# One tile of the first transform, stored as 96 rows to 96 rows instead of four groups of 24

## The chip, the cores and the metric

The kernel runs on one core of one Trainium2 chip. The metric is the device time of one execution in microseconds, lower is better; the time shown for a kernel is the median of its runs. A core has a matrix engine (TensorE, PE in the rows, with PEld for its weight loads), VectorE (DVE), ScalarE (ACT), GpSimd (POOL), a queue engine (SyncE, SP) that here issues nearly all transfers, and 16 DMA engines that carry them. SBUF is the on-chip memory of 128 partitions; a tile's rows lie on partitions.

## What is computed

The input x is [8, 3072, 256]. Along the 3072 positions a real Fourier transform is taken, a complex 256 by 256 matrix mixes the channels, a soft threshold is applied, the inverse transform follows, and the result goes through a feed-forward network with softplus:

```
X = rfft(x, axis=1);  Xr, Xi = X.real, X.imag
Yr = Xr @ w_r - Xi @ w_i + b_r
Yi = Xr @ w_i + Xi @ w_r + b_i
Y  = shrink(Yr) + 1j * shrink(Yi)          # sign(v) * max(|v| - 0.01, 0)
y  = irfft(Y, n=3072, axis=1)
h  = y.reshape(24576, 256) @ w_in          # w_in 256 x 2048
out = softplus(h) @ w_out                  # w_out 2048 x 256
```

## The kernel before

The length 3072 is split as 96 x 32 (N1 x N2). For each of the 8 batches b the spectral part runs in steps that are spread between the feed-forward products of the batch before:

- `s1(b, c)`, c = 0..15: one product with the 96 x 96 matrix `f` gives two of the 32 columns n for all 96 rows, a tile of 96 x 512. ScalarE copies it out of PSUM (L260). Batch 0 keeps all of it on chip, in the tile `a0` (96 partitions, 32 x 256 each). Every other batch stores the tile to a DRAM tensor `a_dr[b]` of [96, 32, 256] (L264, issued in the helper at L100). The first ten tiles of batch 1 come early and go through four slots `a1`, so that tile c may only be copied once the store of tile c - 4 has landed.
- `load_a(b, gp)`, gp = 0..11: fetches two groups g of four rows each, laid out as 128 partitions (four rows times 32 columns n) of 256 values. For batch 0 these are two transfers per step out of `a0` (L273, from SBUF to SBUF, 128 KB each, 24 in all); for the others one transfer out of `a_dr[b]` (L276), beside a table `g1` (L275). The tile `ap` has three buffers, so the transfers of step gp wait until `s3` of step gp - 3 is done.
- `s3` (L287) multiplies by that table, `mix` (L208 to L210) mixes the channels, DVE and POOL apply the threshold, `s4` (L427) begins the inverse transform and its result goes to `d_dr[b]`; `load_d` and `s5` (L455) finish it. Then the feed-forward slots run (`psc`, `pse`, `pso` in the rows).

The columns of `f` do not stand in natural order. They are built on the host as four runs of 24, so that row 24q + g of a tile holds the natural column 4g + q:

```
f = f.reshape(N1, NG, 4).swapaxes(1, 2).reshape(N1, N1)      # NG = 24
```

The four rows of group g are therefore rows g, g + 24, g + 48 and g + 72 of `a0`, and the store to `a_dr` puts them back into natural order, as four groups of 24 rows.

All of these transfers and the streams of weights are issued by SP, one after the other, in an order that a slot plan written out in the kernel fixes (`fill`, `steps`, `later`). In the first 130 us the feed-forward weights are also loaded, split into two parts (`split_w`, L143 to L195) and written back to DRAM (`w_dr`), in between the steps of batch 0. A transfer waits for the one eight places before it on SP to have landed, beside the waits for its data and buffers.

## Time and profile before

| what | us |
|---|---|
| median of 3 runs | 2681.06 |
| lowest and highest run | 2678.23, 2682.66 |
| span of the profiled execution | 2678.0 |
| of it, PE busy | 2603.8 |
| first feed-forward product starts | 131.07 |

The page gives of the profiled execution its span only, 2678.0 us; the lowest run is 0.2 us and the median 3.1 us above it. So what lies around the span is small, and a sum made against the span is carried to the median by adding 3.1 us.

The page's busy shares are averages over the whole span. The first tenth of the run is another regime than the rest, so views of single stretches are read beside it: the table of windows (busy time of each engine in a stretch, the granted clock, the mean busy share of the 16 DMA engines, and what they moved per second), the timeline (instructions in order of time), and the lists of waits.

### The profile page before, as it was taken

Reading aid. Unit: us, or ns where it says so; the run is one execution under the profiler, and the core shown is the slowest. Engines: PE = TensorE matmul, PEld = TensorE weight load, DVE = VectorE, ACT = ScalarE, POOL = GpSimd, SP = SyncE. Lnnn points to the kernel's source line nnn. Section 1 sums busy time; section 2 is a strip of 40 time slices with the busy share of each in tenths; the row PEclk is TensorE's granted clock in tenths of the full one; section 3 lists DMA queues with packets and bytes.
Section 4 is the critical chain, followed back from the end, with each engine's and each line's share of the span. In section 5 each row is a group of like instructions: output and inputs, shape, how many; then the busy total and the mean of one; then the engine's idle time right before and its main releaser. Section 6 shows DMA issues by size and latency. Waiting matters only on the chain.

```text
span 2678.0 us, 36264 instructions
## 1 busy us (share of the span) xinstructions
PE 2603.8 (97%) x13059; PEld 2184.2 (82%) x13059; DVE 1626.2 (61%) x2701; ACT 1719.5 (64%) x3115; POOL 301.3 (11%) x292
## 2 busy tenths in 40 slices
PE   7768999999999999999999999999999999999999
PEld 5546888888888888888888888888888888888887
DVE  3666665666646666566665666556665666645454
ACT  3365666666666666666676666666666666666665
POOL 2432110110101101101011011010010000000000
PEclk8889999999999999999999999999999999999999
DMA  6766556556455565564555644646455455445543
GB/s 191 254 210 206 194 164 198 166 187 193 157 188 178 178 198 170 179 205 156 184 172 172 217 159 153 220 163 198 164 167 191 155 170 188 142 154 183 186 147 110
DMA packets 186116, 479.73 MB, mean 179 GB/s; under 512 B 18097, under 2 KB 86961, under 8 KB 185937
## 3 DMA queue, kind: packets, MB, share of 16 engines
q1 hardware_dynamic: 185376, 476.95, 55.1%
q8 instruction: 103, 1.69, 0.3%
q0 software_dynamic: 560, 0.47, 0.1%
q14 instruction: 77, 0.62, 0.1%
HBM read 390.31 MB, written 83.89 MB: 177 GB/s over the span
## 4 chain that ended last, share of the span: by engine, by line
PE 88%; DVE 2%; DMA 2%; ACT 1%; issue 0%; POOL 0%; SPq 0%; DVEq 0%; ACTq 0%; POOLq 0%
PE pso L208 13%; PE pso L209 12%; PE pso L210 12%; PE psc L208 6%; PE psc L210 6%; PE psc L209 6%; PE pse L208 5%; PE pse L210 5%; PE pse L209 5%; PE psf L455 4%; PE psf L209 4%; PE psf L208 4%; PE psf L210 4%; PE psf L287 2%; DMA w_dr<-wp 1%; DVE shrunk L413 0%
## 5 line engine op out<-in xcount | busy, mean ns | idle before, releaser
L553 DVE TENSOR_TENSOR gl<-t,gh 128x512 fp32r<-128x512 f32 x768 | 533.2, 694 | 349.7 <-ACT gh L547 346.8
L532 ACT COPY t<-psc 128x512 f32<-128x512 f32 x576 | 337.0, 585 | 504.4 <-PE psc L210 502.4
L537 DVE TENSOR_TENSOR t<-pse,t 128x512 f32<-128x512 f32 x576 | 396.2, 688 | 426.9 <-ACT t L532 278.3
L208 PE MATMUL pso<-gh,w 128*128 128x512 f32 x1536 | 616.2, 401 | 0.0
L209 PE MATMUL pso<-gl,w 128*128 128x512 f32 x1536 | 600.0, 391 | 0.0
L210 PE MATMUL pso<-gh,w 128*128 128x512 f32 x1536 | 599.5, 390 | 0.0
L547 ACT CAST gh<-t 128x512 fp32r<-128x512 f32 x768 | 476.8, 621 | 58.2 <-PE pso L210 34.4
L543 ACT ACTIVATE t<-t 128x512 f32<-128x512 f32 x576 | 364.5, 633 | 58.7 <-DVE t L537 58.0
L210 PEld LDWEIGHTS pso<-gh,w 128*128 128x128 f32 x1536 | 288.7, 188 | 62.5
L208 PEld LDWEIGHTS pso<-gh,w 128*128 128x128 f32 x1536 | 290.1, 189 | 54.9
L209 PEld LDWEIGHTS pso<-gl,w 128*128 128x128 f32 x1536 | 290.0, 189 | 51.4
L208 PE MATMUL psc<-y_sb,w 128*128 128x512 f32 x768 | 301.6, 393 | 16.1 <-DMA w<-w_dr 7.8
L210 PE MATMUL psc<-y_sb,w 128*128 128x512 f32 x768 | 300.1, 391 | 0.0
L209 PE MATMUL psc<-y_sb,w 128*128 128x512 f32 x768 | 299.6, 390 | 0.0
L208 PE MATMUL pse<-y_sb,w 128*128 128x512 f32 x576 | 227.8, 396 | 14.4 <-DVE t L537 7.9
L115 POOL TENSOR_TENSOR xl<-xt,xh 96x512 fp32r<-96x512 f32 x102 | 134.1, 1317 | 938.3 <-ACT xh L106 783.6
L209 PE MATMUL pse<-y_sb,w 128*128 128x512 f32 x576 | 225.2, 391 | 0.0
L210 PE MATMUL pse<-y_sb,w 128*128 128x512 f32 x576 | 225.1, 391 | 0.0
L489 POOL TENSOR_TENSOR y_sb<-raw,y_sb 128x512 fp32r<-128x512 f32 x69 | 92.3, 1337 | 1128.5 <-ACT y_sb L486 1124.9
L208 PEld LDWEIGHTS psc<-y_sb,w 128*128 128x128 f32 x768 | 144.5, 188 | 51.0 <-ACT t L532 10.2
L210 PEld LDWEIGHTS psc<-y_sb,w 128*128 128x128 f32 x768 | 144.6, 188 | 31.0
L209 PEld LDWEIGHTS psc<-y_sb,w 128*128 128x128 f32 x768 | 144.6, 188 | 29.7
(131 smaller groups left out, 3637.8 us busy)
## 6 DMA issues: line engine op xcount, KB each, us to landing
w<-w_dr SPq DMA_DIRECT2D x192, 896.0 KB
w<-w_dr SPq DMA_DIRECT2D x192, 512.0 KB
dp<-d_dr SPq DMA_DIRECT2D x80, 384.0 KB
xt<-in_x SPq DMA_DIRECT2D x128, 192.0 KB
d_dr<-d SPq DMA_DIRECT2D x96, 256.0 KB
out_y<-ot SPq DMA_DIRECT2D x96, 256.0 KB
ap<-a_dr SPq DMA_DIRECT2D x84, 256.0 KB
a_dr<-a SPq DMA_DIRECT2D x102, 192.0 KB
```

Of the source, the lines that this page charges most:

```text
L115: (eng or nc.vector).tensor_tensor(out=lo, in0=src, in1=hi.bitcast(F32), op=ALU.subtract)
L208: nc.tensor.matmul(ps, wh, xh, start=start, stop=False, skip_group_check=more)
L209: nc.tensor.matmul(ps, wh, xl, start=False, stop=False, skip_group_check=more)
L210: nc.tensor.matmul(ps, wl, xh, start=False, stop=stop, skip_group_check=more)
L287: nc.tensor.matmul(xv[:, g, k], t[:, g, k * P:(k + 1) * P], g1_t[:, g].rearrange("p (c s) -> p c s", c=2), start=True, stop=True,)
L455: nc.tensor.matmul(ps[:, t - blk * BLK:t - blk * BLK + n], d_sb[b, blk // 2, n2 // 4][0][:, n2 % 4, k * P:(k + 1) * P], d_sb[b, blk // 2, ...
L489: eng.tensor_tensor(out=lo, in0=raw[j], in1=hi.bitcast(F32), op=ALU.subtract)
L532: nc.scalar.copy(t, banks[bank])
L537: nc.vector.tensor_tensor(out=t, in0=banks[bank], in1=t, op=ALU.add)
L543: nc.scalar.activation(t, banks[bank] if bank else t, AF.Softplus)
L547: nc.scalar.copy(gh, ct[key, what])
L553: nc.vector.tensor_tensor(out=gl, in0=ct.pop((key, what)), in1=gh.bitcast(F32), op=ALU.subtract)
```

## The change

Three lines change. The reordering of the columns of `f` is left out, so that row r of a tile is the natural column r. The store of a tile to `a_dr` then writes 96 rows to 96 rows. The four rows of group g in `a0` are now rows 4g to 4g + 3, and `load_a` of batch 0 reads those. The contents of `a_dr` and everything read from it are as before.

```
--- before.py
+++ after.py
         else:
-            store(a_dr[b][:, 2 * c:2 * c + 2, :].rearrange("(g q) n c -> q g n c", q=4), a.rearrange("p (n c) -> p n c", n=2), ("a", b))
+            store(a_dr[b][:, 2 * c:2 * c + 2, :], a.rearrange("p (n c) -> p n c", n=2), ("a", b))
...
             for g in range(2):
-                nc.sync.dma_start(t[:, g, :], a0[2 * gp + g::NG])
+                nc.sync.dma_start(t[:, g, :], a0[4 * (2 * gp + g):4 * (2 * gp + g) + 4])
...
     f[:, 1] = cos(1536 * n1)
-    f = f.reshape(N1, NG, 4).swapaxes(1, 2).reshape(N1, N1)
```

No instruction is added, removed or moved on any engine. On SP, early in the program, the loads of batch 0 (`ap<-a`, L273) and the first stores of batch 1 (`a_dr<-y`, L100) stand in a row like this, with weights, a table and the biases between them:

```order
 L273 DMA ap<-a_79 128x1x256 x6
 L143 DMA w_216<-in_w_in 128x2x512
-L100 DMA a_dr<-y_80 4x24x512
+L100 DMA a_dr<-y_80 96x512
 L273 DMA ap<-a_79 128x1x256 x2
 L749 DMA bias_99<-in_bias 128x512
-L100 DMA a_dr<-y_80 4x24x512 x3
+L100 DMA a_dr<-y_80 96x512 x3
 L273 DMA ap<-a_79 128x1x256 x2
 L749 DMA y_80<-in_g 128x1536
```

Only the shape of the stores differs here; the source rows of the loads differ too, which these rows do not show.

## Rows read from the trace of the kernel before

**Rows 1.** The page: span, then busy time, share and instructions of each engine.

```profile
span 2678.0 us, 36264 instructions
PE 2603.8 (97%) x13059; PEld 2184.2 (82%) x13059; DVE 1626.2 (61%) x2701; ACT 1719.5 (64%) x3115; POOL 301.3 (11%) x292
```

**Rows 2.** Windows: stretch, length, busy of PE, PEld, DVE, ACT, POOL, clock, DMA share, GB/s.

```profile
0.00:280.00 280.00, 217.09 (x1018) 166.56 (x1019) 166.06 (x283) 137.33 (x250) 84.38 (x85) 0.88 0.65 212
280.00:2678.00 2398.00, 2386.71 (x12043) 2017.60 (x12041) 1460.11 (x2418) 1582.12 (x2866) 216.95 (x207) 1.00 0.54 175
```

**Rows 3.** Waits of PE, 20 to 100 us: who for whom, us, times, longest.

```profile
PE psf L287 <- DMA ap<-a: 6.5, 5, 4.3
PE psf L210 <- DVE w L115: 5.6, 2, 4.8
```

**Rows 4.** Windows of short stretches in the first 91 us, columns as in rows 2.

```profile
26.00:30.00 4.00, 2.06 (x8) 1.79 (x8) 0.38 (x1) 0.00 (x0) 0.00 (x0) 0.50 0.28 97
37.00:44.00 7.00, 2.23 (x17) 2.03 (x16) 2.37 (x5) 1.36 (x3) 1.16 (x1) 0.91 0.28 103
3.00:8.00 5.00, 4.10 (x5) 1.48 (x6) 0.00 (x0) 0.94 (x2) 0.00 (x0) 1.00 0.95 261
46.00:47.00 1.00, 1.00 (x7) 1.00 (x7) 0.38 (x1) 0.00 (x0) 0.48 (x1) 0.50 0.99 366
26.00:91.00 65.00, 54.44 (x352) 48.86 (x353) 45.01 (x76) 21.78 (x43) 29.13 (x31) 0.87 0.59 193
```

**Rows 5.** Timeline of SP, 1 to 38 us: start, length, line, transfer, count.

```profile
1.20 17.58 SPq L231 DMA_DIRECT2D xt<-in_x  x20
...
20.84 7.17 SPq L273 DMA_DIRECT2D ap<-a  x6
...
29.41 0.66 SPq L100 DMA_DIRECT2D a_dr<-y  x1
30.39 2.13 SPq L273 DMA_DIRECT2D ap<-a  x2
32.58 2.35 SPq L749 DMA_DIRECT2D bias<-in_bias  x1
35.04 2.98 SPq L100 DMA_DIRECT2D a_dr<-y  x3
```

**Rows 6.** The full list of transfers: count, size of each.

```profile
ap<-a SPq DMA_DIRECT2D x24, 128.0 KB
...
a_dr<-y SPq DMA_DIRECT2D x10, 192.0 KB
```

**Rows 7.** Timeline of PE, `s3` of batch 0 and the first feed-forward product.

```profile
27.83 2.53 PE L287 MATMUL psf<-y,ap 128*128 128x128 f32 x8 [4.25 <-DMA ap<-a]
...
53.49 1.06 PE L287 MATMUL psf<-y,ap 128*128 128x128 f32 x8
...
58.11 1.06 PE L287 MATMUL psf<-y,ap 128*128 128x128 f32 x8
...
90.12 1.33 PE L287 MATMUL psf<-y,ap 128*128 128x128 f32 x8
...
131.07 0.77 PE L208 MATMUL psc<-y_sb,w 128*128 128x512 f32 x1
```

**Rows 8.** Timeline of ACT, 112 to 129 us, with idle time before and its end.

```profile
125.88 0.58 ACT L260 COPY y<-psf 96x512 f32<-96x512 f32 x1 [12.38 <-DMA a_dr<-y]
127.75 0.58 ACT L260 COPY y<-psf 96x512 f32<-96x512 f32 x1 [1.29 <-DMA a_dr<-y]
128.23 0.58 ACT L474 CAST y_sb<-psf 128x512 fp32r<-128x512 f32 x1
```

**Rows 9.** Issue time on SP in ns, least, median, greatest.

```profile
L100 SPq DMA_DIRECT2D a_dr<-a x102: 592/612/925, 155.2 to 2052.1; - x102
...
L231 SPq DMA_DIRECT2D xt<-in_x x128: 312/382/2282, 1.2 to 2027.0; - x128
```

## The prediction

> **What bounds the kernel now.** I read the page first: PE is busy 2603.8 of 2678.0 us [rows 1]. The windows then split the span. From 280 us to the end PE works 2386.7 of 2398 us, so some 11 us are lost in nine tenths of the run; in the first 280 us it works 217.1, so 63 us are lost there [rows 2]. What a transfer costs can therefore show at the start; later there are 11 us to win at the very most, and a transfer would have to become much slower before PE felt it. So the stretch to look at is the one in which batch 0 is read back from `a0`, beside the tiles of batch 1 that are stored early. It runs from 27.8 us, the first product of `s3`, to 90.1 us, its last step; the first feed-forward product follows at 131.1 [rows 7].

> In that stretch PE waits first for the loads `ap<-a`: 6.5 us in five waits, and 5.6 us for a result of DVE [rows 3]. That is little, but the transfers have hardly any slack. The reader should look at the DMA share in the short windows. Between 26 and 30 us, when only the loads issued from 20.8 us on are under way [rows 5], the 16 DMA engines are busy 0.28 on the mean and move 97 GB/s. Between 37 and 44 us, with stores and loads in turn, it is the same picture, 0.28 and 103 GB/s. When tiles of all 128 partitions come in, the share is 0.99 and the pace 366 GB/s [rows 4]. So a load out of `a0` and a store to `a_dr` run on about 4 of the 16 engines, each at some 97/4 = 24 to 103/4 = 25.8 GB/s.

> [...]

> One queue carries all of this. A load of 128 KB [rows 6] takes 131,072 B / 97 GB/s = 1.35 us, and a store of 192 KB takes 196,608 B / 103 GB/s = 1.91 us. From 26 to 91 us, 65 us x 193 GB/s = 12.55 MB move [rows 4]. 24 loads are 3.15 MB of it and 32.4 us; the four stores issued by 38 us [rows 5] are 0.79 MB and 7.6 us; the other 8.61 MB at 366 GB/s are 23.5 us. The sum is 63.5 of 65 us. **The four engines that the loads use are full through the whole stretch.** PE's own step is shorter: where it isn't held up, `s3` of one step follows that of the step before by 58.11 - 53.49 = 4.62 us [rows 7], while two loads and the rest of the queue cost 65/12 = 5.4.

> **The change, part by part.**

> *The reordered table `f`* is made on the host. Nothing of it runs on the chip.

> *The store of a tile* goes from 4 x 24 rows to 96 rows. The nearest row is the load of x, 96 rows of the same size on the same queue, twenty from 1.2 us on [rows 5]: between 3 and 8 us the engines are busy 0.95 at 261 GB/s [rows 4], so 0.75 us for one, against 1.91 now. That saves 1.16 us for each of 102 + 10 stores [rows 6, 9]. The 4 in the full stretch give back 4 x 1.16 = 4.6 us. Two more end a wait of ACT: tiles 8 and 9 of batch 1 are copied at 125.88 and 127.75 us, after 12.4 and 1.3 us of waiting for earlier stores, and the copy that the first feed-forward product's inputs come from is right behind, at 128.23 [rows 8]. Two stores in a row before it give 2 x 1.16 = 2.3 us. The others lie in a stretch where PE loses next to nothing [rows 2]; I take 0 for them, 6 at most. SP needs 612 ns to issue a store and 382 ns for the like-shaped load of x [rows 9]; SP spends its time waiting for PE in that part, so this is worth nothing.

> *The load out of `a0`* keeps its size, its four engines and its place on SP, but its four source rows, until now 24 apart, become neighbours. The trace has no transfer that reads four neighbouring rows, so I bound it. From below: neighbours share nothing, 1.35 us as now. From above: the four engines read through one path, and that path carries what one engine was seen to carry, 24 GB/s: 4 x 1.35 = 5.40 us. The row that decides between the ends is the load of x again. Its engines are busy 0.95 and yet move 261/(16 x 0.95) = 17 GB/s each, where those that load 128 rows move 366/(16 x 0.99) = 23 [rows 4]. Both come from the same memory in long rows; what differs is which partitions they touch. So something on the side of SBUF that belongs to partitions holds engines back, and I take the upper kind of price, with the best pace of an engine seen, 25.8 GB/s, for the path: 131,072 / 25.8 = 5.09 us a load.

> [...]

> With 5.09 us the 24 loads take 122.2 us instead of 32.4, so +89.8, and the stores give back 4.6: the last step of batch 0 comes 85.2 us later. Three buffers of `ap` don't hide that: two loads take 10.2 us a step, against PE's 4.62, and PE's step at half clock, at most 9.2, is still the shorter. What is late next is everything behind the last step; nothing of the feed-forward part can begin before. Two things soften it: the 2.3 us of ACT's wait, and that the splitting of weights and the threshold, which keep DVE busy 45.0 of these 65 us [rows 4], are spread over 150 us and are done when the last step comes. I take 4 us for that, between 0 and 10; a lower clock after the long wait for loads works the other way.

> **Sum.** 85.2 - 2.3 - 4 = +78.9 us on the span of 2678.0, so 2756.9; the median lies 3.1 above the span, so 2760 us. This case's own range, with 4.6 to 5.6 us a load and the softening from 0 to 12, is 2740 to 2780.

> **The rivals.**

> *Neighbours cost nothing.* Then the loads stay at 1.35 us, only the stores count, and the kernel is faster. The price: 4.6 us out of the full queue, of which about half shows, since PE's 4.62 us step is close behind, 2.3 us at ACT, and up to 3 us later: 4 to 8 us, 2675 us. It decides as soon as a load stays under about 1.5 us. For it: now the four engines each read from one row at full pace, so a single row is no obstacle. Against it: the slow engines in the load of x.

> [...]

> *Half the price.* The two loads of a step read two different sets of four rows. If the engines drift apart, so that some are at the first set and some at the second, two paths work at once and a load takes 2.55 us: 61 instead of 32.4, so +28.8 - 4.6 - 6.3 = +18 us, 2699 us. Against it: all four get the loads in the same order and are held up alike.

> *The change doesn't do what it says*: the stores stay on four engines. Then 6.9 us fewer are given back, 2767 us. Against it: the load of x has the same 96 rows and a share of 0.95 [rows 4].

> **How the numbers follow.** Forecast 0.72, neighbours cost nothing 0.16, half the price 0.10, stores unchanged 0.02. The range has to reach down to the half price and leaves out the rival on the other side: 2690 to 2790 us, its upper end for a path slower than one engine. A measurement of this kernel can tell about 0.2%, 5.4 us, from no change. The rival that is faster gives 4 to 8 us, so 0.10 of its 0.16 are faster by more than that and 0.06 lie within; all else is slower, 0.84.

> **What would show it.** Right: the windows of the first 150 us show a DMA share near 0.25 with about 26 instead of 97 GB/s, because four engines are busy and wait for one path; PE's waits for `ap<-a` grow from 6.5 to about 80 us or more; `s3` of batch 0 ends near 175 us, with 10 to 12 us between steps; the first feed-forward product starts near 210; from there to the end the length is as now. The stores, where they run alone, show a share near 0.9 instead of 0.27, and ACT's wait at L260 shrinks. Wrong: `s3` of batch 0 still ends near 90 us, or windows with loads alone still move 97 GB/s. If `s3` ends late but the end moves by much less, the step that failed is that everything behind it shifts by as much.

## The result

The changed kernel takes 2712.6 us, the median of four runs, against 2680.9 us before: a ratio of 1.0117, 95% interval 1.0105 to 1.013. It is slower by 31.7 us, where 79 were forecast. The sign is right, but the size is less than half of what was said. The time lies inside the stated range of 2690 to 2790 us only because that range was drawn down to the rival "half the price"; the forecast's own range was 2740 to 2780.

The profiled execution of the changed kernel has a span of 2705.4 us. Its windows (stretch, length, busy time of PE, PEld, DVE, ACT and POOL with counts, clock, DMA share, GB/s) answer to [rows 2, 4]:

```profile
26.00:30.00 4.00, 0.91 (x4) 0.93 (x4) 0.69 (x1) 0.38 (x1) 0.00 (x0) 0.67 0.24 50
52.40:53.60 1.20, 1.20 (x6) 1.20 (x7) 1.17 (x3) 0.00 (x0) 0.48 (x1) 0.50 0.22 26
62.50:65.50 3.00, 3.00 (x23) 2.52 (x22) 2.93 (x4) 2.70 (x5) 1.35 (x1) 1.00 0.23 52
26.00:125.00 99.00, 61.41 (x355) 53.45 (x356) 43.59 (x77) 21.95 (x44) 28.96 (x31) 0.79 0.45 128
310.00:2705.00 2395.00, 2385.71 (x12046) 2018.60 (x12044) 1461.17 (x2420) 1582.71 (x2867) 217.20 (x207) 1.00 0.54 175
```

From 26 to 30 us the loads out of `a0` are alone on the queue, as before. The share is still that of four busy engines, 0.24 against 0.28, but 50 GB/s move instead of 97 [rows 4]. For a short while, from 52.4 to 53.6 us, the pace is 26 GB/s, that of one engine; at other times it is twice that. The whole stretch that took 65 us for 193 GB/s now takes 99 us at 128 GB/s: nearly the same bytes, 12.5 and 12.7 MB. From 310 us on, PE loses 9.3 of 2395 us, no more than before [rows 2].

PE's waits between 20 and 130 us (who for whom, us in total, times, longest), to be set beside [rows 3]:

```profile
PE psf L287 <- DMA ap<-a: 32.0, 14, 4.6
PE psf L210 <- DVE w L115: 7.0, 1, 7.0
```

And PE's timeline (start, length, instruction, idle before and what ended it), beside [rows 7]: in 14 places PE now waits for the load of one half of an `s3`, where it waited in 5, the last step starts 31.7 us later (121.84 against 90.12), and the first feed-forward product 32.8 us later (163.91 against 131.07).

```profile
29.09 1.20 PE L287 MATMUL psf<-y,ap 128*128 128x128 f32 x4 [4.56 <-DMA ap<-a]
33.02 1.22 PE L287 MATMUL psf<-y,ap 128*128 128x128 f32 x4 [2.73 <-DMA ap<-a]
...
111.07 0.68 PE L287 MATMUL psf<-y,ap 128*128 128x128 f32 x4 [2.77 <-DMA ap<-a]
115.80 1.22 PE L287 MATMUL psf<-y,ap 128*128 128x128 f32 x4 [4.04 <-DMA ap<-a]
...
121.84 0.61 PE L287 MATMUL psf<-y,ap 128*128 128x128 f32 x4
...
163.91 0.77 PE L208 MATMUL psc<-y_sb,w 128*128 128x512 f32 x1
```

So the place and the kind of the cost are as forecast. What has to be explained is why a load that should cost 5.1 us costs much less. With the prediction's own terms, 23.5 us for the other transfers and 3.0 us for the four stores, the 99 us leave (99 - 26.5) / 24 = 3.0 us a load.

### The profile page after: what moved, and what is told of

Its sections match the earlier page's. It is cut to its first block, busy times and chain, and to the rows that moved or that the text cites. A ratio compares the mean times of both kernels' runs of the same rounds, so it can differ in the third digit from the quotient of the medians.

```text
span 2705.4 us, 36264 instructions
## 1 busy us (share of the span) xinstructions
PE 2609.3 (96%) x13059; PEld 2189.8 (81%) x13059; DVE 1625.6 (60%) x2701; ACT 1719.5 (64%) x3115; POOL 301.4 (11%) x292
## 4 chain that ended last, share of the span: by engine, by line
PE 88%; DVE 2%; DMA 1%; ACT 1%; issue 0%; POOL 0%; SPq 0%; DVEq 0%; ACTq 0%; POOLq 0%
PE pso L208 13%; PE pso L209 12%; PE pso L210 12%; PE psc L208 6%; PE psc L210 6%; PE psc L209 6%; PE pse L208 5%; PE pse L210 5%; PE pse L209 5%; PE psf L455 4%; PE psf L209 4%; PE psf L208 4%; PE psf L210 4%; PE psf L287 3%; DVE shrunk L413 0%; DMA w<-in_w_in 0%
```

## The experiments

Three theories went in. **A**: four neighbouring rows share one path that carries what one engine carries, about 26 GB/s; engines that run apart from each other get to different loads, whose rows lie on different paths, and that is where the price fell from 5 to 3 us. **B**: a path simply carries 50 GB/s. **C**: the load isn't the cause.

### The load by itself

A kernel that does nothing but move data: one load, then seven in a row, for several choices of four rows, each block after the end of the one before. A block has a name, the first row of each of its loads, and the distance between the four rows of a load.

```
block("near", [0] * 7, 1)                        # rows 0, 1, 2, 3, seven times
block("far", [0] * 7, 24)                        # rows 0, 24, 48, 72
block("near_next", [0, 4, 0, 4, 0, 4, 0], 1)     # 0-3 and 4-7 in turn
block("near_over", [0, 32, 0, 32, 0, 32, 0], 1)  # 0-3 and 32-35 in turn
block("two_apart", ..., 2); four_apart: 4; eight_apart: 8; most_apart: 32
```

> The disputed cost by itself: a kernel that leaves the whole computation out and only moves data, with nothing beside it. Loads of 128 KB from four rows of SBUF to 128 partitions, in blocks, each block waiting for the one before: one load, then seven in a row, from four neighbouring rows (near), from rows 24 apart (far), from neighbours in turn from two sets (rows 0 to 3 and 4 to 7: near_next; rows 0 to 3 and 32 to 35: near_over), and from rows 2, 4, 8 and 32 apart; then seven stores of 192 KB as four groups of 24 rows and as 96 rows. Theory A (four neighbours share one path of about 26 GB/s, the pace of one engine, and in the changed kernel engines that drift onto the other set of a step use a second path): near 5.1 us a load, so about 36 us for seven, far 1.35 us, so about 10; near_next between, 2.6 to 4 us a load; 2 apart 2.6, 4 apart and more 1.35. [...] Theory B (a path carries about 50 GB/s, whatever the engines do): near 2.6 us a load, 18 us for seven, near_next and near_over the same. Theory C (the load is not what became slow): near as far, about 10 us. Stores: 1.9 us each in groups, 0.5 to 0.75 us as 96 rows.

DVE reads one column of every tile when it has landed; its timeline gives the landings, here the first and the last of seven, neighbours and then rows 24 apart:

```profile
30.80 0.15 DVE L38 COPY flag<-near 128x1 f32<-128x1 f32 x1 [7.11 <-DMA near<-src]
...
62.00 0.15 DVE L38 COPY flag<-near 128x1 f32<-128x1 f32 x1 [4.98 <-DMA near<-src]
...
65.46 0.15 DVE L38 COPY flag<-far 128x1 f32<-128x1 f32 x1 [3.25 <-DMA far<-src]
...
73.95 0.15 DVE L38 COPY flag<-far 128x1 f32<-128x1 f32 x1 [1.25 <-DMA far<-src]
```

Six loads from the same neighbours take 31.20 us, **5.20 us each**; six from rows 24 apart 8.49 us, 1.42 each. The windows of the blocks (here busy times of DVE and POOL, clock, DMA share, GB/s), in the order near, far, near_next, near_over, two, four, eight and 32 apart:

```profile
31.00:62.00 31.00, 0.77 (x6) 0.00 (x0) 1.00 0.21 25
65.50:73.50 8.00, 0.89 (x6) 0.00 (x0) 1.00 0.26 90
81.00:100.00 19.00, 0.86 (x6) 0.00 (x0) 1.00 0.22 39
108.00:138.00 30.00, 0.92 (x6) 0.00 (x0) 1.00 0.22 26
143.00:157.00 14.00, 0.82 (x6) 0.00 (x0) 1.00 0.23 53
161.00:170.00 9.00, 0.92 (x6) 0.00 (x0) 1.00 0.25 82
174.00:182.00 8.00, 0.82 (x6) 0.00 (x0) 1.00 0.26 89
187.00:203.00 16.00, 0.92 (x6) 0.00 (x0) 1.00 0.23 47
```

The share hardly differs, 0.21 to 0.26: in each block four engines count as busy, whether they move 25 or 90 GB/s. Read with theory A, one path carries 25 to 26 GB/s (four neighbours), two carry 53 (rows 2 apart) and four 82 to 90 (rows 4, 8 and 24 apart). B and C fall here. With two sets of neighbours in turn (0 to 3 and 4 to 7) the pace is 39 GB/s, and it grows within the block: the gaps between landings are 5.0, 4.6 and 4.3 us, then 1.4, 1.5 and 3.1. With rows 0 to 3 and 32 to 35 in turn there is no such gain: 26 GB/s, and gaps of 4.7 to 5.3 us to the last.

The same run stores seven tiles in four groups of 24 rows and then seven as 96 rows. The grouped ones land 1.9 to 2.1 us apart and the others, queued up behind them, 0.5 us apart (from the semaphore records that are explained further down); the prediction's sum had 1.91 and 0.75.

### Each half of the change alone

A second order of the columns of `f`, used by batch 0 alone, separates the two halves. The edits that follow are against the changed kernel and cut to their main lines; both also load the second table (72 KB instead of 36 KB) and let batch 0 use it. The store half:

```
+    f_0 = f[:, np.arange(N1).reshape(NG, 4).T.reshape(-1)]
...
-                nc.sync.dma_start(t[:, g, :], a0[4 * (2 * gp + g):4 * (2 * gp + g) + 4])
+                nc.sync.dma_start(t[:, g, :], a0[2 * gp + g::NG])
```

> The store half of the change alone: the table f has a second order of columns that batch 0 alone uses, so batch 0's rows stay 24 apart while the other batches are stored as 96 rows to 96 rows. It loads a table of 72 KB instead of 36 KB at the start. Theories A and B: the cost goes, and what is left is the stores' gain, 4 to 8 us by the prediction, so 2673 to 2677 us. Theory C (the slower part comes from the stores or from the natural order of f): about 2710 us.

2670.7 us, ratio 0.9963 (0.995 to 0.9975): **faster than both kernels**, by 9.9 us or 0.37% (from the ratio) against the kernel before, a little more than the 4 to 8 us that the prediction gave the stores. The last step of batch 0 begins at 88.4 us:

```profile
88.37 1.06 PE L287 MATMUL psf<-y,ap 128*128 128x128 f32 x8
...
130.07 0.77 PE L208 MATMUL psc<-y_sb,w 128*128 128x512 f32 x1
```

The load half keeps natural order for batch 0 and goes back to four groups of 24 for the rest:

```
+    f_0 = f[:, np.arange(N1)]
+    f = f[:, np.arange(N1).reshape(NG, 4).T.reshape(-1)]
...
-            store(a_dr[b][:, 2 * c:2 * c + 2, :], a.rearrange(...), ("a", b))
+            store(a_dr[b][:, 2 * c:2 * c + 2, :].rearrange("(g q) n c -> q g n c", q=4), a.rearrange(...), ("a", b))
```

> The load half alone: batch 0 in natural order, its four rows of a group neighbours, while the other batches keep the reordered columns and the store in four groups of 24. Theories A and B: as slow as the whole change or a little slower, since the stores no longer help: 2714 to 2720 us, last step of batch 0 at 120 to 128 us. Theory C: 2681 us.

2719.2 us, ratio 1.014 (1.0125 to 1.0155), 37.5 us slower. PE waits for the loads as in the whole change, and the last step begins at 121.4 us:

```profile
PE psf L287 <- DMA ap<-a: 27.5, 13, 4.6
PE psf L210 <- DVE w L115: 9.4, 2, 8.8
```

So the whole cost is the load's. The halves add up to +27.6 us where the change has +31.7; with intervals of some 3 to 4 us to either side that difference isn't clear of the measurement.

### Which rows share a path, in the kernel itself

The same kernel with batch 0's rows placed in other ways, by the order of the columns of `f` that batch 0 uses; the stores are those of the change. near_over bears on `e4_pair32`: with sets 32 rows apart in turn a load took 5.06 us, so engines that run apart within a step should win nothing there. In short:

```
e3_apart2:  t[:, g, :] <- rows r, r + 2, r + 4, r + 6        (two paths)
e3_apart4:  t[:, g, :] <- rows r, r + 4, r + 8, r + 12       (four paths)
e4_pair32:  rows 4p to 4p + 3, and for the second group of a step 4p + 32 to 4p + 35, in 8 of 12 steps
```

> The whole change with batch 0's rows in another order: the four rows of a group are 2 apart (rows 8p, 8p+2, 8p+4, 8p+6 and the odd ones between), so they lie on two paths by theory A; stores as in the changed kernel. The loads alone took 2.45 us each in a row in m1. Theory A: with 2.45 us a load against 1.42, 24 x 1.03 = 25 us more transfer time than the store half alone, of which PE's own steps hide a few: 2685 to 2697 us. If only direct neighbours cost, 2671 us; if any group within eight rows costs the same as neighbours, 2712 us.

> As e3_apart2 with rows 4 apart (16p, 16p+4, 16p+8, 16p+12 and the sets between): four paths by theory A, 1.42 us a load in m1. Theory A: as the store half alone, 2668 to 2674 us, faster than the kernel before. If what matters is that rows are far apart, not which path they take: 2685 us or more.

> The whole change, but for eight of the twelve steps of batch 0 the two groups of a step lie 32 rows apart (rows 4p to 4p+3 and 4p+32 to 4p+35) instead of next to each other; everything else is as in the changed kernel, but for the larger table at the start. [...] Theory A: up to 8 x 2 x (5.1 - 2.9) = 35 us more than the changed kernel, 2725 to 2748 us; less if engines drift on to the next step's loads. Theory B, or a path of four rows alone: as the changed kernel, 2705 to 2718 us.

| four rows of a group | one load in a row of seven | ratio of the kernel | interval |
|---|---|---|---|
| 24 apart (store half alone) | 1.42 us | 0.9963 | 0.995 to 0.9975 |
| 4 apart | 1.56 us | 0.9969 | 0.9957 to 0.9981 |
| 2 apart | 2.46 us | 1.0031 | 1.0019 to 1.0042 |
| neighbours (the change) | 5.20 us | 1.0117 | 1.0105 to 1.013 |
| neighbours, pairs 32 apart | 5.06 us (near_over) | 1.0181 | 1.0166 to 1.0197 |

The middle column is the time between the first and the seventh landing over six, from the first experiment; for rows 4 apart it is 1.56 us, not the 1.42 of the expectation, which is that of rows 24 apart. Rows 4 apart are as good as rows 24 apart, so distance as such isn't needed, only four paths. Rows 2 apart cost 0.68% more than the store half, 18 us: 24 loads at 1.04 us more would be 25, of which PE's steps hide a part. The last row is the test of the drift: its loads are as slow by themselves as those of the change, but where a step's second load uses the same path as its first (26 GB/s in turn, near_over), running apart within a step is of no use, and the kernel loses another 17 us. Its first window and its waits, beside those of the change:

```profile
26.00:30.00 4.00, 1.19 (x4) 0.93 (x4) 0.18 (x1) 0.00 (x0) 0.00 (x0) 0.50 0.22 29
...
PE psf L288 <- DMA ap<-a: 46.8, 17, 5.5
```

29 GB/s where the change had 50, and 46.8 us of waits where it had 32.0. A path of 50 GB/s, or one that only four rows share, would have left it at the time of the change.

### The 24 loads in their order

Again only data moves: the 24 loads of batch 0 one after the other, without and with a transfer of 512 KB after every second one. A row has a name, the first row of each load, the distance of its four rows, and whether transfers come in between.

```
walk("near", [4 * g for g in range(24)], 1)                  # as in the change
walk("pairs", ..., 1); walk("far", list(range(24)), 24)      # as in e4_pair32; as before
walk("near_beside", ..., 1, True)                            # 512 KB to 128 rows after every second load
```

> Only data moves here too (the whole computation is left out): the 24 loads of batch 0 in the order of the kernel, one after the other on the queue, from four neighbouring rows each (near), in the order of e4 with eight pairs 32 rows apart (pairs), from rows 24 apart (far); then the same three with a transfer of 512 KB to 128 rows after every second load (beside), as the kernel has them on average. Theory A (one path of about 25 GB/s per four neighbours, 5.2 us a load when the engines run alike, and drift onto other loads' rows as the engines get apart): near begins at about 5 us a load and gets faster as it goes, 24 loads in 60 to 80 us instead of 125; pairs slower than near, 75 to 105 us; far 24 x 1.42 = 34 us. With transfers beside: 12 x 1.4 = 17 us more for far; near between 75 and 100 us. Theory D (the engines stay alike, and the kernel's 2.9 us a load comes from gaps that other transfers left): near 125 us alone.

The landings of the first and second, the fifth, and the last load, then those of the first and the last for the others (near, pairs, far, near_beside, pairs_beside, far_beside):

```profile
19.96 0.15 DVE L40 COPY flag<-near 128x1 f32<-128x1 f32 x1 [18.57 <-DMA near<-src]
24.59 0.15 DVE L40 COPY flag<-near 128x1 f32<-128x1 f32 x1 [4.48 <-DMA near<-src]
...
32.45 0.15 DVE L40 COPY flag<-near 128x1 f32<-128x1 f32 x1 [1.48 <-DMA near<-src]
...
68.05 0.15 DVE L40 COPY flag<-near 128x1 f32<-128x1 f32 x1 [1.89 <-DMA near<-src]
...
75.38 0.15 DVE L40 COPY flag<-pairs 128x1 f32<-128x1 f32 x1 [7.12 <-DMA pairs<-src]
...
135.99 0.15 DVE L40 COPY flag<-pairs 128x1 f32<-128x1 f32 x1 [1.79 <-DMA pairs<-src]
...
139.35 0.15 DVE L40 COPY flag<-far 128x1 f32<-128x1 f32 x1 [3.15 <-DMA far<-src]
...
171.68 0.15 DVE L40 COPY flag<-far 128x1 f32<-128x1 f32 x1 [1.20 <-DMA far<-src]
...
178.69 0.15 DVE L40 COPY flag<-near_beside 128x1 f32<-128x1 f32 x1 [6.80 <-DMA near_beside<-src]
...
264.33 0.15 DVE L40 COPY flag<-near_beside 128x1 f32<-128x1 f32 x1 [2.87 <-DMA near_beside<-src]
...
271.81 0.15 DVE L40 COPY flag<-pairs_beside 128x1 f32<-128x1 f32 x1 [7.26 <-DMA pairs_beside<-src]
...
371.69 0.15 DVE L40 COPY flag<-pairs_beside 128x1 f32<-128x1 f32 x1 [3.16 <-DMA pairs_beside<-src]
...
375.08 0.15 DVE L40 COPY flag<-far_beside 128x1 f32<-128x1 f32 x1 [3.18 <-DMA far_beside<-src]
...
423.09 0.15 DVE L40 COPY flag<-far_beside 128x1 f32<-128x1 f32 x1 [1.95 <-DMA far_beside<-src]
```

The second near load comes 4.6 us after the first, close to the full price, the fifth only 1.6 us after the fourth, and all 24 are there 48.1 us after the first: 2.1 us each, where far ones take 32.3 us. I had expected 60 to 80, so the engines run apart faster than I thought. The pairs alone take 60.6 us where 75 to 105 were expected; they begin at 4.6 to 5.3 us a load, so running apart helps them too, only later. With the transfers between, near takes 85.6 us, pairs 99.9 and far 48.0. The near ones lose 37.6 us to the far ones; in the kernel the change loses 41 to the store half alone (1.0117 against 0.9963). The pairs lose 51.9, in the kernel 58 (1.0181). A near load in such company costs 1.4 + 37.6/23 = 3.0 us, the figure found in the trace of the change.

Do the engines run apart, or does this only look like it? The kept trace can tell. Beside what the views print, it holds the time of every update that a transfer makes to its semaphore, the counter that those who wait for it watch. A load out of four rows leaves one near its issue and four more when data lands, a transfer to 128 rows sixteen; I take the four as the ends of its four engines' parts. In the near row without transfers, in us from the start of the span:

| load | its four parts end at | first to last |
|---|---|---|
| 1st | 19.74, 19.75, 19.82, 19.93 | 0.2 |
| 2nd | 23.37, 24.05, 24.40, 24.57 | 1.2 |
| 3rd | 24.72, 26.84, 28.39, 28.40 | 3.7 |
| 5th | 27.43, 29.58, 31.77, 32.42 | 5.0 |

The first part of the fifth load ends before the last part of the third: the engines are at different loads. In the first experiment, where all seven loads read the same four rows, or rows 0 to 3 and 32 to 35 in turn, the four parts of every load end within 0.2 to 0.6 us of each other. In the changed kernel the parts of a load of batch 0 end up to 6.9 us apart (3.7 on the mean), in the kernel before up to 3.2 (1.7 on the mean). And the first six of these loads, which stand next to each other on SP, land 3.0 us apart there and 1.4 us apart before.

Why is it 3.0 in company and 2.1 alone? One more kernel put fewer, and smaller, transfers between the loads:

```
walk("near_four", near, 1, 4)        # 512 KB after every fourth load
walk("near_eight", near, 1, 8)       # after every eighth
walk("near_small", near, 1, 2, 128)  # 64 KB after every second
```

> Only data moves (the whole computation is left out). The 24 loads of m2 from four neighbouring rows, and from rows 24 apart beside them for comparison, with a transfer of 512 KB to 128 rows after every fourth load (four), after every eighth (eight), and one of 64 KB after every second (small). In m2 a near load cost 2.1 us alone and, measured against the far ones, 3.0 us with 512 KB after every second load. Theory E (a transfer on all engines brings the four that run apart together again): the fewer such transfers, the cheaper: about 2.6 us a near load with four between, 2.3 with eight, and with the small transfer about 3.0, since it comes as often as the large one. Theory F (only the time that large transfers take away from the overlap counts): about 2.6 and 2.3 too, but 2.1 to 2.3 with the small one.

First and last landing of the small case, near and far:

```profile
237.89 0.15 DVE L40 COPY flag<-near_small 128x1 f32<-128x1 f32 x1 [6.83 <-DMA near_small<-src]
...
323.44 0.15 DVE L40 COPY flag<-near_small 128x1 f32<-128x1 f32 x1 [3.40 <-DMA near_small<-src]
...
326.82 0.15 DVE L40 COPY flag<-far_small 128x1 f32<-128x1 f32 x1 [3.16 <-DMA far_small<-src]
...
360.37 0.15 DVE L40 COPY flag<-far_small 128x1 f32<-128x1 f32 x1 [1.22 <-DMA far_small<-src]
```

The near row takes 85.6 us with the small transfers as it did with the large ones, although the far row loses 14.4 us less to the small ones (33.6 against 48.0). With a transfer after every fourth load the near row takes 64.6 us, after every eighth 57.5, with none 48.1; the far rows take 39.6, 35.6 and 32.3. So what counts is how often a transfer on all the engines comes in between, and not how much it moves. That decides for theory E against F, by which a near load would have cost 2.1 to 2.3 us with the small ones. E's own figure for that case, about 3.0, was too low: 1.4 + 52.0/23 = 3.7 us, measured against the far row.

The semaphore records fit E as well. With 512 KB between, the four parts of a load end 3.3 us apart on the mean just ahead of a transfer and 1.8 us just behind it; with 64 KB 2.9 and 1.6; after every fourth load 4.6 and 2.5. In the near row without transfers they stay about 3.5 us apart from the sixth load on. A transfer on all the engines brings the four closer together, though not all the way. By which means it does so stays open.

### Where the stores' gain lies

The prediction put the stores' gain at the start and took 0 for the later ones. A kernel that stores the first ten tiles of batch 1 in four groups still, and the other 102 as 96 rows:

```
+            dst = a_dr[b][:, 2 * c:2 * c + 2, :]
+            if early:
+                dst = dst.rearrange("(g q) n c -> q g n c", q=4)
```

> Part of the store half: the 102 later tiles are stored as 96 rows to 96 rows, the first ten tiles of batch 1 still as four groups of 24, and batch 0 keeps rows 24 apart. If the gain of the store half (11 us) lies in the first ten, as the prediction had it (6.9 us there, 0 to 6 later): 2677 to 2681 us, the rest of the run as before. If the later stores give the larger part: 2673 to 2675 us.

2675.7 us, ratio 0.9984 (0.9975 to 0.9993): the later stores give 4.3 us, between 2 and 7, and the first ten the rest of the 9.9, about 5 to 6, with some 4 us of uncertainty. It falls just below the 2677 to 2681 us of the prediction and just above the 2673 to 2675 of the other case. Its trace shows PE idle for 8.8 of 2390 us after 280 us, some 2.5 us less than before [rows 2], so a part of these 4 us is seen as idle time there; the rest I can't place:

```profile
280.00:2670.00 2390.00, 2381.23 (x12028) 2015.45 (x12026) 1458.25 (x2415) 1579.81 (x2861) 216.83 (x207) 1.00 0.54 175
```

## Why the prediction was right in kind and wrong in size

**What bounds the kernel: right in the main.** The first 280 us are where PE loses time, and the loads out of `a0` run on four engines (a DMA share of 0.28 before [rows 4] and 0.24 now). With nothing added to any other engine's work, 1.65 us more for each of 24 loads moved the last step by 31.7 us. But the queue of the kernel before was not full through the whole stretch: from 53.49 to 71.97 us five steps follow each other at PE's own 4.62 us with no wait for a load [rows 7], and faster stores alone brought the last step forward by 1.75 us (88.37 against 90.12), and not at all with rows 4 apart (90.10), where 4.6 had been added up.

**The price of one load: right.** 5.09 us were taken from the pace of one engine and the clue in the load of x; 5.20 were measured where nothing else was on the queue and the rows stayed the same. The forecast's reason for preferring the upper bound held for these loads: it is the partitions that count, 5.20 us against 1.42 for the same 128 KB on about as many engines (0.21 and 0.26). That the load of x is slow for the same reason was not tested.

**The sum of 24 loads: wrong.** The step that failed is "24 loads take 122.2 us instead of 32.4, so +89.8". It multiplied the price of a load that has the queue's engines in step by 24. The engines don't stay in step: each goes on to the next load, on another path, when its own part is done, and the parts of one load ended up to 6.9 us apart in the changed kernel. In the row of the kernel a load costs 3.0 us, so the term is 24 x (3.0 - 1.35) = +40 us, not +90. This mechanism stood in the prediction as the rival "half the price", with a chance of 0.10 and 2.55 us a load, and was put aside because "all four get the loads in the same order and are held up alike". That argument is what the second load of a row does (4.6 us) and not what the fifth does (1.6 us). The trace of before could not decide it, since it has no load that reads four neighbouring rows; but the rival deserved a chance as large as the forecast's, and a range of its own up to the full price.

**The stores: about right in size, wrong in place.** 4.6 us were put to the full queue and 2.3 to the wait of ACT, 6.9 in all ahead of the first feed-forward product. The store half alone is 9.9 us faster, but that product starts only 1.0 us earlier in its trace (130.07 against 131.07), and the kernel with late stores alone, which up to there is like the one before, starts it at 129.10: single profiles differ by that much. By 280 us PE has done 222.1 us of work with the store half, against 217.1 before [rows 2], so about 5 of the 9.7 us between the two spans lie ahead of 280 us, most of them behind that product, where the prediction took 0 and allowed 6:

```profile
0.00:280.00 280.00, 222.09 (x1043) 171.47 (x1044) 171.50 (x290) 142.19 (x259) 84.41 (x85) 0.88 0.66 218
```

ACT's wait itself ended as described: in the changed kernel tiles 8 and 9 are copied together, and the next copy follows 0.96 us after the first of them starts instead of 2.35 [rows 8]. But the first feed-forward product was not waiting for it. PE works on `s5` without a pause until that product begins, in the kernel before and with the store half alone, where the copy at L474 comes 3.5 us earlier (124.69 against 128.23):

```profile
122.55 8.71 PE L455 MATMUL psf<-dp 96*128 96x96 f32 x40 [0.68 <-DMA dp<-d_dr]
...
121.54 8.71 PE L455 MATMUL psf<-dp 96*128 96x96 f32 x40 [0.59 <-DMA dp<-d_dr]
```

The copies in the changed kernel:

```profile
158.03 1.07 ACT L260 COPY y<-psf 96x512 f32<-96x512 f32 x2 [10.65 <-DMA a_dr<-y]
158.99 0.59 ACT L474 CAST y_sb<-psf 128x512 fp32r<-128x512 f32 x1
```

**The softening: wrong.** 4 us were to come back because the splitting of weights is done by then. From the last step to the first feed-forward product it is 42.1 us now and 40.9 before [rows 7]: neither the 4 us nor ACT's 2.3 came back there. The lower clock that was to work the other way is seen: 0.79 on the mean over the 99 us, against 0.87 over the 65 [rows 4]. From that product to the end of the span the run is 5 us shorter (2541.5 against 2546.9 us); with the stores alone changed that part is 8.7 us shorter (2538.2), so the stores are the likely cause.

With 3.0 us a load, 4.6 us for the early stores and none for softening, the same sum gives +35 us for the last step; 31.7 were measured. That is no independent proof, since the 3.0 was read from the same stretch of the same trace; that the row of bare loads gave 3.0 as well is better evidence.

## What to carry to other kernels

When a transfer touches few partitions, look at which ones: four neighbouring rows gave less than a third of the pace of four rows that lie 4 or 24 apart (25 against 82 to 90 GB/s), and the DMA share shows about four engines busy in both cases (0.21 and 0.25 to 0.26), so read the GB/s beside the share. An order of rows that looks needlessly shuffled may serve two transfers at once; give each its own order where that is free, as here, where the store's natural rows are worth 0.4% and the load's shuffled ones 1.5%. And a price measured for one transfer isn't the price of a row of them when several engines share the work (here 5.2 us with the engines in step, 2.1 to 3.0 with them apart): bound the row from both sides, engines in step and engines apart.

## What the runs showed that I had not expected

In a row of loads that read different sets of neighbours, the engines slowed each other only until they had run apart: 24 such loads went from 4.6 us for the second to 2.1 us on the mean, where rows 0 to 3 over and over took 5.2. A transfer on all engines in between took part of that back, a small one as much as a large one: the row of 24 grew from 48.1 to 85.6 us with 64 KB after every second load and with 512 KB alike, although for loads from rows 24 apart 64 KB added little more than 1 us (33.6 against 32.3) and 512 KB 15.7.
